# Routing in two segments instead of three, with the value sums, the stores of x and the small steps rearranged, in a fused attention and expert kernel

## The chip, the cores and the metric

The kernel runs on one core of a Trainium2 chip. Its engines work side by side, each through its own list of instructions in order: TensorE (PE, whose weight loads the profile calls PEld), VectorE (DVE), ScalarE (ACT), GpSimd (POOL) and SyncE (SP, which issues most transfers here). The metric is the device time of one execution in microseconds (us). Of the kernel before, three timed runs are given.

## What is computed

Attention over a local window and block summaries, and behind it a mixture of eight experts. The core of the reference (B = 4 batches, H = 8 heads, S = 768 positions, head size 64, so rows of 512):

```python
k_sum = k.reshape(B, H, nb, block, D).max(axis=3)      # blocks of 32
v_sum = v.reshape(B, H, nb, block, D).mean(axis=3)
scores_l = scale * q @ k.T, kept where |i - j| < 16
scores_s = scale * q @ k_sum.T + log(32)
a = softmax(concat(scores_l, scores_s))
x = a @ concat(v, v_sum)                               # 4 x 768 rows of 512
for b, s in order:
    fresh_e = argmax(x[b, s] @ w_gate)
    e = fresh_e if s == 0 or sigmoid(x[b, s] @ w_local) < 0.5 else prev_e
    p = softmax(x[b, s] @ w_gate)
    out[b, s] = p[e] * (relu(x[b, s] @ w1[e]) @ w2[e])
```

A row's expert can be that of the row ahead of it, so a routing scan runs through each batch. With the given inputs all 768 rows of batch 0 go to one expert, those of batch 1 to a second, batch 2 and most of batch 3 to a third (1400 rows), 135 to a fourth and one row to a fifth: 24 blocks of up to 128 rows, and two small remainders.

## The kernel before, in words

**Attention.** The 32 pairs of heads and batches are cut into 16 head pairs n (4 batches by 4) with two groups g each, so 32 groups G, G = 2n + g, and `attention` runs a software pipeline over G. In group G PE makes the scores (`s_mm`, L300 and L306, into two banks of PSUM called bs), then in odd groups the gate's product of the values (`gate_v`, L265), in even groups its transposes (`gate_t`, L273), then the transposes of the probabilities of group G - 2 (`t_stage`, L326), and the value product of group G - 3 (`a_mm`, L337, into the one bank ba). The sums of the values over blocks are a small product too (`sum_v`, L251): from n = 2 on it is made in even groups and written to spare columns of the scores' bank, copied by ACT to vs (L253) and spread by POOL into the value tile vw (`spread_v`, L258). DVE takes the maximum of the scores (nm, L312), block maxima or block sums of the next k or v (L218, L222), and normalizes: `a_norm` writes dn and xs (L352, L353), which empties ba. ACT makes the exponentials (L316) and copies. POOL also copies windows of k (L244), folds the next v (`fold_v`, L229) and scales summaries (L247).

**Loads and stores.** SP issues the loads of kp, q, vt and vw in program order, two or three pairs ahead. When the fourth head pair of a batch is normalized, `a_norm` also has SP store the rows of x to `x_dram` (L357), two stores of 876 KB a batch. The store waits for xs, and what follows on SP waits behind it.

**Small steps.** Routing is a chain of small instructions, written as generators that yield before each: "DVE", "LONG" (a large DVE step), "PE" or "PE late" (a product), "ACT", "WAIT". `later` puts a chain in the list `steps`; `small(n)`, called three times in each group with 3, 2 and 4, takes that many steps, PE's only after two or four calls since the step ahead. Behind attention `flow` does the same by a model of time.

**Routing.** `SEG` cuts the batches in three segments: 0, then 1 and 2, then 3. `route(k)` finds each row's expert (L539 to L579), counts and ranks (L582 to L606), and makes the selection matrix A (L626). It runs for segment 0 from group 10 on, for segment 1 from group 26 on, for the last behind attention. `early(j)` picks two blocks of 128 rows each ahead of the rest: j = 0 from batch 0, j = 1 and 2 from batches 0 to 2, all of expert e0, the one with the most rows in batch 0; j = 3 is for e1, which `second` chooses. `gate_p` makes the rows' weights, with one exponential on ACT between DVE steps (L697 to L702). `finish` places the remaining blocks, makes the list `words` (which expert each slot needs, L1001 and L1006) and the row numbers (L932), first for slots 8 to 11 and then for the rest, and the weights by row (L1023).

**Experts.** Slots are blocks of rows; `pair` runs two blocks of one expert: 96 products for the first layer (L1159 to L1161), 48 for the second (L1078 to L1080), each number in two parts. The first four pairs are the early blocks. The weights of e0 are fetched and split in attention's last groups (wst, L1032, L1036, L1039, L1044); those of e1 are fetched behind attention (stg), and split in the second layer of the third pair. Rows come by an indirect transfer (`gather`, L1050) and are transposed (L1061) into xT.

## Time and profile before

| | |
|---|---|
| median of 3 runs | 459.29 us (458.85 to 460.34) |
| the profiled execution | 458.1 us |
| its span, first to last instruction | 456.3 us |
| mean granted clock of PE | 0.979 |
| busy PE, DVE, POOL, ACT | 418.9, 233.8, 197.3, 183.1 us |
| moved by DMA | 91.28 MB, 200 GB/s over the span |
| attention, up to the first expert product | 137.74 us |
| experts, up to the last product | 440.7 us |

Busy times of an engine are shares of the span in which an instruction of it runs; matmuls overlap, so PE can be busy without being at its peak. In the rows below a time is counted from the span's start; an instruction's row names what it writes and reads (out<-in), and in brackets the idle time of its engine ahead of it with what ended that.

### The profile page before, as it was taken

How to read it: one execution, taken by the hardware profiler on the slowest of the kernel's cores; microseconds unless marked ns; L12 is line 12 of the kernel's file. 1: busy time of each engine (PE TensorE's matmuls, PEld its weight loads, DVE VectorE, ACT ScalarE, POOL GpSimd, SP SyncE). 2: the span in 40 equal slices, each digit the busy share in tenths (PEclk: the TensorE clock that was granted, in tenths of full speed). 3: DMA queues.
4: the chain of work that ended last, by engine and by line, in shares of the span. 5: the costliest groups of instructions: out<-in, count | busy, mean ns of one | idle time of the engine just before them, and what ended most of it. 6: DMA issues, size and time to landing. Idle time of an engine off the chain costs nothing. (4 is left out here: it accounts for less than half of the span.)

```text
span 456.3 us, 11758 instructions
## 1 busy us (share of the span) xinstructions
PE 418.9 (92%) x4329; PEld 358.0 (78%) x4329; DVE 233.8 (51%) x559; ACT 183.1 (40%) x470; POOL 197.3 (43%) x288
## 2 busy tenths in 40 slices
PE   7799898987879999999999999999999999999960
PEld 7577676675658889898989888798988989898840
DVE  4667789797688866668221222226322721214520
ACT  3978776765774222137222111016313721204510
POOL 4497676675574320208621211205820931112930
PEclk9999999989999999999999999999999999999995
DMA  8998998979846470202993246201951671120680
GB/s 306 417 381 311 386 351 264 412 287 337 319 134 218 158 310 1 82 19 87 338 406 115 75 178 225 86 15 28 322 186 39 224 252 70 28 76 25 198 302 32
DMA packets 22854, 91.28 MB, mean 200 GB/s; under 512 B 2767, under 2 KB 3281, under 8 KB 19185
## 3 DMA queue, kind: packets, MB, share of 16 engines
q1 hardware_dynamic: 18176, 74.63, 44.0%
q0 software_dynamic: 4448, 15.42, 10.3%
q8 instruction: 41, 0.67, 0.6%
q14 instruction: 45, 0.36, 0.3%
q10 hardware_dynamic: 144, 0.20, 0.1%
HBM read 76.77 MB, written 13.60 MB: 198 GB/s over the span
## 5 line engine op out<-in xcount | busy, mean ns | idle before, releaser
L1159 PE MATMUL bs<-xT,h 128*128 128x256 f32 x352 | 101.0, 287 | 0.0
L1160 PE MATMUL bs<-xT,h 128*128 128x256 f32 x352 | 99.8, 283 | 0.9 <-DVE xT L1056 0.9
L1161 PE MATMUL bs<-xT,l 128*128 128x256 f32 x352 | 99.6, 283 | 0.0
L1050 POOL DMA_INDIRECT xg<-x_dram,gidx x30 | 32.9, 1096 | 107.5 <-PE bt L1061 39.6
L1078 PE MATMUL ba<-h,hT 128*128 128x512 f32 x176 | 71.5, 406 | 0.3
L1165 ACT ACTIVATE hT<-bs 128x512 fp32r<-128x512 f32 x44 | 26.3, 597 | 112.8 <-PE bs L1161 110.8
L1167 DVE SCALAR_TENSOR_TENSOR hT<-bs,hT 128x512 fp32r<-128x512 f32 x44 | 30.4, 691 | 78.5 <-ACT hT L1165 67.3
L1080 PE MATMUL ba<-h,hT 128*128 128x512 f32 x176 | 68.9, 391 | 0.0
L1079 PE MATMUL ba<-l,hT 128*128 128x512 f32 x176 | 68.8, 391 | 0.0
L1160 PEld LDWEIGHTS bs<-xT,h 128*128 128x128 f32 x352 | 67.4, 192 | 1.7 <-DVE xT L1056 1.4
L1159 PEld LDWEIGHTS bs<-xT,h 128*128 128x128 f32 x352 | 67.4, 191 | 1.8 <-issue 1.2
L1161 PEld LDWEIGHTS bs<-xT,l 128*128 128x128 f32 x352 | 67.4, 192 | 0.2 <-DVE l L1039 0.2
L316 ACT ACTIVATE pr<-bs,nm 128x120 f32<-128x120 f32 x192 | 52.1, 383 | 29.1 <-DVE nm L312 29.0
L1091 POOL DMA_INDIRECT out_dram<-yo,sidx x24 | 25.9, 1078 | 62.1 <-DVE yo L1090 22.2
L1044 POOL TENSOR_TENSOR l<-stg,h 128x256 fp32r<-128x256 f32 x48 | 41.7, 901 | 8.2 <-ACT h L1036 7.6
L258 POOL COPY vw<-vs 24x438 f32<-24x438 f32 x64 | 36.0, 602 | 10.3 <-ACT vs L253 8.3
L337 PE MATMUL ba<-vw,pt 121*64 121x74 f32 x768 | 33.2, 235 | 6.3 <-DVE xs L353 3.8
L312 DVE TENSOR_REDUCE nm<-bs 128x6 f32<-128x720 f32 x32 | 28.7, 900 | 19.6 <-ACT vs L253 18.3
L1080 PEld LDWEIGHTS ba<-h,hT 128*128 128x128 f32 x176 | 33.0, 188 | 7.3
L1078 PEld LDWEIGHTS ba<-h,hT 128*128 128x128 f32 x176 | 33.1, 188 | 6.9 <-ACTq L1330 0.6
L337 PEld LDWEIGHTS ba<-vw,pt 121*64 121x64 f32 x768 | 28.4, 140 | 12.2 <-issue 4.7
L1079 PEld LDWEIGHTS ba<-l,hT 128*128 128x128 f32 x176 | 33.2, 189 | 5.6
(269 smaller groups left out, 658.1 us busy)
## 6 DMA issues: line engine op xcount, KB each, us to landing
stg<-in_w SPq DMA_DIRECT2D x20, 1024.0 KB, 7.6
vw<-in_vW SPq DMA_DIRECT2D x16, 888.0 KB, 7.6
raw<-in_w SPq DMA_DIRECT2D x8, 1024.0 KB, 7.2
x_dram<-xs SPq DMA_DIRECT2D x8, 876.0 KB, 4.8
kp<-in_kT SPq DMA_DIRECT2D x16, 384.0 KB, 5.9
q<-in_qT SPq DMA_DIRECT2D x16, 384.0 KB, 6.9
vt<-in_vT SPq DMA_DIRECT2D x16, 384.0 KB, 7.4
wst<-in_w SPq DMA_DIRECT2D x8, 512.0 KB, 5.8
```

The source lines that it names most:

```text
L258: nc.gpsimd.tensor_copy(out=vf[n % 3][WL:W, t:t + NW // 4, 1:1 + PW], in_=vs.to_broadcast([NB, NW // 4, PW]))
L316: nc.scalar.activation(out=pr[:, h, u, :], in_=sp[:, h, u, :], func=AF.Exp, bias=nm[:, h, u:u + 1], scale=1.0)
L337: nc.tensor.matmul(out=ap[64 * c:64 * c + 64, u, h, :], lhsT=pt[0:W + 1, h, u, 64 * c:64 * c + 64], rhs=vw[n % 3][0:W + 1, 2 * (NG * g + u ...
L1044: eng.tensor_tensor(out=lo[:, p], in0=src[:, p], in1=hi[:, p].bitcast(F32), op=ALU.subtract)
L1050: self.nc.gpsimd.indirect_dma_start(out=t.rearrange("p a d -> p (a d)"), out_offset=None, in_=rows, in_offset=bass.IndirectOffsetOnAxis(ap ...
L1078: nc.tensor.matmul(out=ps, lhsT=ah, rhs=wh, start=first, stop=False)
L1079: nc.tensor.matmul(out=ps, lhsT=ah, rhs=wl, start=False, stop=False)
L1080: nc.tensor.matmul(out=ps, lhsT=al, rhs=wh, start=False, stop=last)
L1159: nc.tensor.matmul(out=ps[:, j], lhsT=wh, rhs=xh, start=(k == 0), stop=False)
L1160: nc.tensor.matmul(out=ps[:, j], lhsT=wh, rhs=xl, start=False, stop=False)
L1161: nc.tensor.matmul(out=ps[:, j], lhsT=wl, rhs=xh, start=False, stop=(k == KT - 1))
L1167: nc.vector.scalar_tensor_tensor(out=l, in0=ps, scalar=0.0, in1=h.bitcast(F32), op0=ALU.max, op1=ALU.subtract)
```

## The change

- **Two segments.** `SEG` is batch 0, then batches 1 to 3. `early` is one chain for six blocks (EARLY = 6), all of e0 and all from batch 0, with one product for their row numbers and one for their weights. `second`, `early_p`, e1 and the first part of the row numbers are gone; the next expert's weights are fetched when `words` are there, and slots from 6 on are ordinary ones. The route of batches 1 to 3 starts behind attention, followed at once by `finish`.
- **Value sums.** From n = 2 on the product is made in odd groups, behind the gate's product and into the same bank; ACT copies both.
- **Stores of x.** `a_norm` notes the store; it is issued one group later, behind that group's loads (for the last batch in the same group).
- **Small steps.** `small` takes a budget in us: for even groups 0.5, 0.2 and 0.3, for odd ones 0.7, 0.4 and 0.3, from group 28 on 0.9, 0.5 and 0.4. A step costs 0.29, a LONG one 0.95, PE, ACT and WAIT 0.1. "ACT" waits four calls like "PE late", and both routes use "PE late".

```diff
-SEG = ((0, 1), (1, 3), (3, 4))
+SEG = ((0, 1), (1, B))
-EARLY = 8
-FIRST = 12
+EARLY = 6
-ON_PE = {"PE": 2, "PE late": 4}
+ON_PE = {"PE": 2, "PE late": 4, "ACT": 4}
+TIME, MORE = ((0.5, 0.2, 0.3), (0.7, 0.4, 0.3), (0.9, 0.5, 0.4)), 28
...
             def gate_v(n):
...
+                sums = m[:, 256:256 + 2 * DG]
+                if n > 1:
+                    sum_mm(n, sums)
                 gs = gss[n] = wk.tile([P, GW], F32, name="gs", bufs=2)
                 nc.scalar.copy(out=gs, in_=m[:, 0:GW])
+                if n > 1:
+                    sum_copy(n, sums)
...
                 if p == NP - 1:
                     t = b * NU + NG * g
-                    nc.sync.dma_start(out=self.x_dram[:, t:t + NG, :], in_=x.rearrange("p u a d -> p u (a d)"))
+                    stores.append((G + LA + (0 if b == B - 1 else 1), t, x))
...
-                if 2 * GP < G < last_g and g == 0 or G == 2 * GP + 1:
-                    sum_v(n, spare)
...
                 if G < last_g:
                     s_exp(G)
-                    self.small(3, True)
+                    self.small(TIME[groups[G][1] if G < MORE else GP][0], True)
...
+                while stores and stores[0][0] <= G:
+                    _, t, x = stores.pop(0)
+                    nc.sync.dma_start(out=self.x_dram[:, t:t + NG, :], in_=x.rearrange("p u a d -> p u (a d)"))
                 tick(G, 5)
                 tick(G, 1)
...
-            self.credit -= 4 if head[0] == "LONG" else 1
+            self.credit -= 0.95 if head[0] == "LONG" else 0.1 if head[0] in ON_PE or head[0] == "WAIT" else 0.29
...
-        on_pe = "PE late" if k == 0 else "PE"
+        on_pe = "PE late"
...
-        yield from rows(EARLY, FIRST)
...
         self.have_words()
-        yield from rows(FIRST, COLS)
-        yield from self.gate_p(B - 1, B)
-        yield from self.until(*(("weights", b) for b, _ in SEG[:2]))
+        yield from rows(EARLY, COLS)
+        yield from self.gate_p(*SEG[1])
...
-        after = ([self.early(0), self.also(self.early_p(*SEG[0], 0))],
-                 [self.early(1), self.early(2), self.also(self.early_p(*SEG[1], 1, 2, 3)), self.second()])
-        for k in range(NS - 1):
-            at(GP * NP * SEG[k][1] + 2, 1, lambda k=k: self.later(self.route(k), *after[k]))
+        at(GP * NP * SEG[0][1] + 2, 1, lambda: self.later(self.route(0), self.early()))
...
             def have_words():
                 st["words"] = reg(COLS + EARLY - 2, (ENG.SP,), E - 1)
-                refills()
+                for w in range(2):
+                    refill(w, st["words"])
```

Three places of the order. SP around the two stores of batch 0's rows, before and after:

```order
L186 DMA vw_144<-in_vW 128x1776
L357 DMA x_dram<-xs 128x3x584
L174 DMA kp_136<-in_kT 128x768
L182 DMA q_133<-in_qT 128x768
L357 DMA x_dram<-xs 128x3x584
L178 DMA vt_140<-in_vT 128x768
L186 DMA vw_142<-in_vW 128x1776
```

```order
L182 DMA vw_139<-in_vW 128x1776
L170 DMA kp_131<-in_kT 128x768
L178 DMA q_128<-in_qT 128x768
L174 DMA vt_135<-in_vT 128x768
L182 DMA vw_137<-in_vW 128x1776
L452 DMA x_dram<-xs 128x3x584
L170 DMA kp_130<-in_kT 128x768
L178 DMA q_129<-in_qT 128x768
L452 DMA x_dram<-xs 128x3x584
L174 DMA vt_136<-in_vT 128x768
```

Each store (x_dram) stood ahead of the loads of its group; now it stands behind the loads of the next group.

DVE in groups 26 and 27, before and after (nm is the maximum of the scores that opens a group on DVE; l_all collects the gate's inputs):

```order
L359 TENSOR_REDUCE l_all<-xs 128x27
L539 TENSOR_REDUCE mx_2186<-l_all 128x12
L542 TENSOR_TENSOR eq_2192<-l_all,mx_2186 128x96
L544 TENSOR_TENSOR eq_2192<-eq_2192,c_82 128x96
L547 TENSOR_REDUCE rv_2195<-eq_2192 128x12
L312 TENSOR_REDUCE nm<-bs 128x6
L550 TENSOR_TENSOR sv_2197<-c_82,rv_2195 128x12
L553 SCALAR_TENSOR_TENSOR val_2242<-l_all,sv_2197 128x12
L555 COPY val_2242<-sv_2197 1x2
```

```order
L321 TENSOR_REDUCE nm<-bs 128x6
L663 TENSOR_REDUCE gmx_2153<-l_all 128x6
L666 TENSOR_TENSOR ex_2201<-l_all,gmx_2153 128x48
L218 TENSOR_REDUCE va<-vf 128x24
L361 RECIPROCAL dn<-ba 128x6
L362 TENSOR_TENSOR xs<-ba,dn 128x3x146
L321 TENSOR_REDUCE nm<-bs 128x6
L671 TENSOR_REDUCE sm_2204<-ex_2201 128x6
L673 TENSOR_SCALAR sm_2204<-sm_2204 128x6
L214 TENSOR_REDUCE ks<-kp_131 128x24
L361 RECIPROCAL dn<-ba 128x6
```

The second route's first four steps stood between l_all and nm of group 27; now one step of batch 0's early blocks stands there, and its exponential's sum (L671) comes a group behind the input of it (L666).

PE around the product for `words` (L1001 before, L947 after), in the second pair of the experts:

```order
L1080 MATMUL ba_3465<-h_118,hT 128x512
L1078 MATMUL ba_3465<-h_118,hT 128x512
L1079 MATMUL ba_3465<-l_120,hT 128x512
L1080 MATMUL ba_3465<-h_118,hT 128x512
L1001 MATMUL bt<-ident,w_3501 1x46 x2
L1159 MATMUL bs<-xT,h_117 128x256
L1160 MATMUL bs<-xT,h_117 128x256
L1161 MATMUL bs<-xT,l_119 128x256
L1159 MATMUL bs<-xT,h_117 128x256
```

```order
L1104 MATMUL bs<-xT,h_112 128x256
L1105 MATMUL bs<-xT,h_112 128x256
L1106 MATMUL bs<-xT,l_114 128x256
L947 MATMUL bt<-ident,w_3082 1x46 x2
L1104 MATMUL bs<-xT,h_112 128x256
L1105 MATMUL bs<-xT,h_112 128x256
L1106 MATMUL bs<-xT,l_114 128x256
L1104 MATMUL bs<-xT,h_112 128x256
L1105 MATMUL bs<-xT,h_112 128x256
```

It stood behind the last product of the second pair (ba); now it stands ahead of that pair's second layer, six products before the end of the first (bs).

## Rows read from the trace of the kernel before

**Rows 1.** Busy us (instructions) of each engine by stage, TensorE clock, DMA share, GB/s
```profile
29.24:42.43 13.19, 13.00 (x262) 10.05 (x259) 9.70 (x18) 11.05 (x42) 11.51 (x23) 1.00 0.88 314
42.43:84.52 42.09, 37.41 (x729) 28.52 (x726) 36.05 (x88) 30.66 (x117) 26.53 (x52) 1.00 0.94 342
84.52:105.24 20.72, 18.21 (x331) 14.30 (x328) 16.14 (x40) 13.96 (x54) 16.84 (x31) 0.92 0.84 323
105.24:125.52 20.28, 15.61 (x270) 11.86 (x267) 14.48 (x33) 13.21 (x44) 9.91 (x18) 0.92 0.90 341
125.52:137.74 12.22, 9.64 (x165) 7.43 (x162) 10.79 (x27) 9.07 (x27) 8.61 (x11) 1.00 0.39 131
137.74:240.19 102.45, 101.55 (x803) 91.45 (x800) 64.41 (x237) 31.00 (x45) 35.47 (x37) 1.00 0.50 182
```

**Rows 2.** PE timeline, clean groups: start us, busy us, instructions, idle before and its releaser
```profile
29.24 0.35 PE L300 MATMUL bs<-me 64*64 64x360 bf16 x4
...
34.55 0.43 PE L251 MATMUL bs<-wgi,va 128*24 128x146 f32 x2
...
42.43 0.35 PE L300 MATMUL bs<-me 64*64 64x360 bf16 x4
```

**Rows 3.** PE timeline, the same columns: long waits of attention
```profile
75.35 1.00 PE L337 MATMUL ba<-vw,pt 121*64 121x74 f32 x24 [1.20 <-DVE xs L353]
...
92.60 1.75 PE L337 MATMUL ba<-vw,pt 121*64 121x74 f32 x24 [1.31 <-DVE xs L353]
...
111.34 0.27 PE L558 MATMUL bt<-ident,val 128*12 128x128 f32 x1 [2.73 <-DVE val L555]
```

**Rows 4.** DVE timeline: the gate's sum, behind ACT
```profile
90.13 0.20 DVE L702 TENSOR_REDUCE sm<-ex 128x6 f32<-128x48 f32 x1 [1.60 <-ACT ex L698]
```

**Rows 5.** Stages again, columns as in group 1, behind PE's two long waits
```profile
92.00:96.00 4.00, 3.40 (x55) 3.06 (x56) 3.76 (x11) 1.38 (x6) 3.83 (x9) 0.57 0.98 366
112.00:116.00 4.00, 4.00 (x44) 3.00 (x38) 1.14 (x3) 1.77 (x7) 0.66 (x2) 0.57 1.04 422
```

**Rows 6.** SP's DMA issues: a store of x and the next load
```profile
44.57 0.38 SPq L357 DMA_DIRECT2D x_dram<-xs  x1
45.04 0.44 SPq L178 DMA_DIRECT2D vt<-in_vT  x1
```

**Rows 7.** POOL timeline: the fold of the next values, the last spread
```profile
51.44 1.16 POOL L229 TENSOR_TENSOR vf<-vt 128x192 f32<-128x192 f32 x2 [3.48 <-DMA vt<-in_vT]
...
132.37 3.69 POOL L258 COPY vw<-vs 24x438 f32<-24x438 f32 x4
```

**Rows 8.** A stage with DMA at its fastest, columns as in group 1
```profile
53.00:56.30 3.30, 2.85 (x61) 2.61 (x62) 2.35 (x6) 2.85 (x12) 2.58 (x6) 1.00 1.06 435
```

**Rows 9.** Who waited for whom: us in total, times, longest
```profile
DVE nm L312 <- ACT vs L253: 18.3, 12, 2.9
```

**Rows 10.** PE timeline: a wait in attention's tail
```profile
133.90 0.60 PE L337 MATMUL ba<-vw,pt 121*64 121x74 f32 x10 [0.45 <-POOL vw L258]
```

**Rows 11.** PE timeline: starts of an expert pair without routing and of its successor
```profile
381.03 0.28 PE L1159 MATMUL bs<-xT,h 128*128 128x256 f32 x1
...
404.42 0.28 PE L1159 MATMUL bs<-xT,h 128*128 128x256 f32 x1
```

**Rows 12.** PE by line, first four expert pairs: count, busy us, mean ns, idle
```profile
L775 PE MATMUL bt<-ebp,A 128*128 128x6 bf16 x54 | 1.8, 166 | 0.0
L746 PE MATMUL bt<-ebt,A 128*128 128x4 bf16 x54 | 1.8, 165 | 0.0
L932 PE MATMUL bt<-bt,A 128*128 128x8 bf16 (+1 forms) x48 | 1.7, 180 | 0.0
```

**Rows 13.** DVE timeline: the last route's first step, and the words
```profile
140.90 0.20 DVE L539 TENSOR_REDUCE mx<-l_all 128x6 f32<-128x48 f32 x1
...
191.25 0.24 DVE L1006 CAST words<-bt 1x92 int32<-1x92 f32 x1 [2.18 <-PE bt L1001]
```

**Rows 14.** ACT timeline: the first cast of fetched expert weights
```profile
204.38 1.04 ACT L1036 CAST h<-stg 128x1024 fp32r<-128x1024 f32 x1
```

## The prediction

> **What bounds the kernel now.** I read the stages first [rows 1]. From 137.74 us to 440.7 us TensorE multiplies for the experts without a pause (101.55 busy in 102.45 us of the first four pairs), so that part shrinks only by work that PE loses. The 15.6 us behind it are the last rows' way out; nothing there is touched. Before 137.74 us stands attention, 32 groups. Where nothing disturbs it, PE is the bound there too: group 7 starts at 29.24 and group 11 at 42.43, four groups in 13.19 us, 3.30 us each, with 13.00 us of PE busy [rows 1, 2]. From group 11 on it is slower. Against 3.30 us a group, the stretch 42.43 to 84.52 (11 groups) is 5.8 us too long, 84.52 to 105.24 (5 groups) 4.2, 105.24 to 125.52 (4 groups) 7.1. The last stretch, 125.52 to 137.74, would cost 9.0 us without waits (a group of 3.3 and, an estimate at the same pace, 5.7 for what is left of three more groups and the first expert transposes); it takes 12.2, 3.2 too many. In all 20.3 us of excess [rows 1], and this is what the change can win in attention.

> Who is late in it? PE's waits show it [rows 3]: the value products wait for DVE's xs (1.20 us at 75.35, 1.31 us at 92.60), since one bank holds them and DVE must empty it first; the transpose of val stands at 111.34 after 2.73 us, for a DVE step of the second routing. Behind DVE is routing: DVE is busy 9.70 of 13.19 us in the clean stretch, 36.05 of 42.09 us in the next, 9.4 us above the clean rate (0.735 of 36.3 us), just what 11 groups leave free (0.265 of 36.3 is 9.6). At 90.13 DVE also stands 1.60 us for the gate's exponentials on ACT [rows 4]. After the two long waits PE's clock is granted at 0.57, one stretch of 4 us each [rows 5], which loses 0.43 of 4, some 1.7 us; those slow groups belong to the 4.2 and the 7.1.

> **Part by part.** *Routing in two segments.* Of the work between groups 26 and 31, the route of batches 1 and 2 goes to the time behind attention. In its place stays the tail of batch 0's chain, which the order shows now ending in group 31. So the stretch of 7.1 loses the 2.73 us wait and the 1.7 us of slow clock behind it, and the PE steps of that route; what stays is the splitting of the weights, with four casts on ACT and one long subtraction on DVE in the last groups. I leave 2.5 of 7.1 (bounds 0, if ACT has room, and 7.1, if casts were the whole cause; nearer to the low end, since 4.4 have names that go).

> *Small steps in us.* Before, nine steps fit in a group; now 1.0 us in even and 1.4 us in odd groups (1.8 from group 28 on), at 0.29 us a step: three or four, and five. Batch 0's route and early blocks took 9.4 us of DVE above the clean rate up to 84.52 and 4.0 (16.14 less 0.735 of 16.5) up to 105.24, 13.4 in all; spread over the 20 groups from 11 to 30, that is 0.67 us a group against 0.87 free. DVE thus stays behind PE instead of in front of it. Of the 5.8 I leave 2.0: 1.2 us for the chain's own 18 products on PE (twelve like L775 at 1.8 / 54 = 0.033 us [rows 12], the other six at 0.13, an estimate between that and the 0.27 of the one at 111.34 [rows 3]) and 0.8 of waits; bounds 1.2 and 5.8. Of the 4.2 I leave 0.5, since the wait for ACT gets four calls of distance and the clock has no reason to fall; bounds 0 and 4.2.

> *Stores behind loads.* Now the store waits on SP for xs and holds vt's load behind it: issued at 44.57 and 45.04 [rows 6], landed when POOL, 3.48 us idle, folds it at 51.44 [rows 7]. Afterwards loads go first and the store waits for nothing. I price it at nothing by itself: PE's long waits name DVE, not a transfer. The cover is the distance from the fold to the products that need it, and POOL's slack, 1.68 us in the clean 13.19; without it the bound would be the 3.48 us for each of three batches, 10.4. The traffic fits: the clean stretch moves 314 GB/s at a share of 0.88 [rows 1], stores add 0.9 MB twice in 26.4 us, 66 GB/s, to 380, and up to 435 GB/s are seen [rows 8].

> *Value sums beside the gate's product.* The two matmuls move from even to odd groups, 0.36 us of PE either way (0.43 busy, next work 0.36 later [rows 2]), and write into the gate's bank. nm no longer waits for ACT's copy of vs, which was 18.3 us in 12 waits [rows 9]. I price this at nothing: 34.55 in rows 2 is such a group, and PE runs on at 3.30 us with that wait inside. Bounds: 0 and the 1.5 us for each of 12 groups. [...] The trace has the wait and no PE idle behind it, so the row decides.

> *Tail.* POOL spreads the last sums at 132.37 in 3.69 us, after its share of the weights, and PE waits for it at 133.90 [rows 7, 10]. The order leaves this as it is: I keep 3.0 of 3.2 (bounds 0 and 3.2).

> Attention thus keeps 2.0 + 0.5 + 2.5 + 3.0 = 8.0 of 20.3 us: 12.3 us gained.

> *Behind attention.* A pair without routing takes 23.39 us (381.03 to 404.42) [rows 11]; the first four take 102.45, 8.9 more, of which 0.9 is the first wait for xT. The rest is routing's own matmuls and what each breaks. The change drops there all of L775 and L746, 108 products and 3.6 us of PE, and the narrower of the two sets of 24 in L932, which take 1.7 together and that one some 0.7 [rows 12]; the route and the wide products stay. That is 4.3, less 0.1 for wider products: 4.2 us gained (bounds 3.6, if the sets merge at the cost of both, and 8.0, all of the excess but the wait). The three new early pairs use the weights that are there; the fourth needs the next expert's. Its fetch now follows the words. In the order the words' product stands six products ahead of the second layer of the second pair, some 35.7 us into the stage (25.0 for the first pair, 90 products at 0.12); the first cast of fetched weights comes, as now, in the second layer of the third pair (204.38 is 66.6 us in, after the change some 61) [rows 14]. 25 us for four megabytes, 11 at 380 GB/s: no wait.

> **Sum.** The profiled execution took 458.1 us, a span of 456.3 and 1.8 around it, 1.2 below the median of the runs. 458.1 - 12.3 - 4.2 = **441.6 us**.

> **Rivals.** *(a) Attention stays bound by DVE, ACT or DMA.* The steps per group are fewer, but in groups 28 to 31 the budget rises while ACT casts, and the same bytes go through in less time. For it: DVE works at 86% of the span from 42.43 on, and DMA shares of 0.94 in that stretch. Against it: 0.67 us against 0.87 free, and 314 GB/s where the clean pace is held. If only the second routing's waits go (4.4 us) and 1 us elsewhere, 458.1 - 5.4 - 4.2 = 448.5 us.

> *(b) The other side: PE waits in line for the single routing chain.* PE takes its work in order, so a words' product that stands 35.7 us into the stage stops the experts if DVE's chain is not done. Now 50.4 us pass from the first step of that chain to the words (140.90 to 191.25) [rows 13]. At that pace from 3 us on it is done at 53.4; PE stands 17.7 us, and slow clock behind such a wait adds 1.7: 441.6 + 19.4 = 461.0 us, slower. It decides from a chain of 33 us on, a microsecond for each microsecond. Against it: three early chains and a second choice of expert were interleaved with it and are gone, and the DVE steps that the order lists ahead of the words, at their durations in the trace, sum to about 34 us from the start of the stage, other work of the experts among them.

> *(c) The stores do count.* Then up to 10 us of attention are won by that part instead of by the steps; the excess is the same, and its floor is 1.2 us: 458.1 - 19.1 - 4.2 = 434.8 us.

> **How the numbers follow.** Forecast 0.72, (a) 0.16, (b) 0.06, (c) 0.06. The range reaches nearly to (c), and 2 us past (a), for casts that cost all of the 7.1: 435.5 to 451. Outside it are (b) and the far ends. A measurement of this kernel tells some 0.3% from no change (458.85 to 460.34 in three runs). Faster 0.92 (forecast, a, c, less some of a's far end), same 0.03, slower 0.05.

> **What would show it.** Right: groups 11 to 27 at 3.3 to 3.5 us and no clock of 0.57; PE's wait for val gone; the first expert product some 12 us earlier; the first four expert pairs near 98 us; no PE wait at the words. Wrong: value products still waiting for xs (steps), POOL still waiting for vt with PE idle behind it (stores), PE idle ahead of the words' product (b), or a DMA share of 1 through the last twelve groups.

## The result, and the profile after

The changed kernel takes 445.89 us (444.76 to 447.59), the kernel before 459.07 us in the same comparison: a ratio of 0.9722, 95% interval 0.9671 to 0.9774. That is 13.2 us less where 16.5 were forecast. The profiled execution took 444.76 us, a span of 443.0 and 1.8 around it, 13.3 less than the one of before. Of these, 10.1 lie ahead of the first expert product and 3.4 between it and PE's last product; the way out is 0.3 longer.

The stages of the kernel after, in the windows that begin with the same groups as [rows 1]; columns as there:

```profile
29.24:42.06 12.82, 12.82 (x262) 10.34 (x259) 9.70 (x17) 11.32 (x44) 11.37 (x24) 1.00 0.96 355
42.06:80.22 38.16, 36.17 (x724) 28.64 (x721) 31.06 (x74) 31.41 (x117) 27.26 (x55) 1.00 1.00 367
80.22:97.82 17.60, 16.07 (x328) 13.22 (x325) 15.20 (x36) 14.09 (x54) 13.03 (x26) 1.00 0.98 374
97.82:115.66 17.84, 13.47 (x264) 10.49 (x260) 13.42 (x33) 12.38 (x45) 10.81 (x20) 1.00 1.00 370
115.66:127.60 11.94, 9.92 (x172) 7.85 (x169) 8.66 (x18) 9.72 (x30) 9.09 (x13) 1.00 0.53 169
127.60:227.79 100.19, 98.89 (x678) 88.73 (x674) 60.90 (x162) 30.24 (x43) 36.78 (x38) 1.00 0.50 188
```

The clock is 1.00 in every stretch, where [rows 5] had 0.57. DVE is busy 31.06 us of the second stretch instead of 36.05. The DMA share, 0.84 to 0.94 before, is now 0.98 to 1.00 in the middle of attention: the same bytes go through in less time.

PE's timeline of two groups that nothing disturbs, the counterpart of [rows 2]:

```profile
42.06 0.35 PE L309 MATMUL bs<-me 64*64 64x360 bf16 x4
42.24 0.79 PE L315 MATMUL bs<-kb,q 64*64 64x120 f32 x24
42.95 0.59 PE L268 MATMUL bt<-vt,wg 128*32 128x224 f32 x8
43.35 0.41 PE L247 MATMUL bt<-wgi,va 128*24 128x146 f32 x2
43.70 0.87 PE L335 MATMUL bt<-ident,pr 128*120 128x128 f32 x6
44.50 1.00 PE L346 MATMUL ba<-vw,pt 121*64 121x74 f32 x24
45.42 0.35 PE L309 MATMUL bs<-me 64*64 64x360 bf16 x4
...
48.36 0.35 PE L309 MATMUL bs<-me 64*64 64x360 bf16 x4
```

An odd group takes 3.36 us and an even one 2.94: 6.30 us a pair, where before each took 3.30. The forecast held the clean pace for fixed; it is not.

Waits of the kernel after, from 29 to 128 us: who waited for what, us in total, times, longest:

```profile
DVE xs L362 <- DMA x_dram<-xs: 7.7, 3, 3.3
...
ACT pr L325 <- DVE nm L321: 4.0, 3, 3.3
...
POOL vf L225 <- DMA vt<-in_vT: 2.5, 2, 1.5
```

POOL's wait for V, one of whose cases is in [rows 7], was 11.5 us in all from 29 to 138 us in the kernel before; it has shrunk to 2.5, and that of [rows 9] is gone. But the first line is new: the normalisation that writes a tile of x waits until an earlier store of x has landed. One of the three, on DVE, then ACT, then PE:

```profile
109.39 0.62 DVE L362 TENSOR_TENSOR xs<-ba,dn 128x438 f32<-128x438 f32 x1 [3.31 <-DMA x_dram<-xs]
```

```profile
112.43 1.62 ACT L325 ACTIVATE pr<-bs,nm 128x120 f32<-128x120 f32 x6 [3.26 <-DVE nm L321]
```

```profile
110.26 1.00 PE L346 MATMUL ba<-vw,pt 121*64 121x74 f32 x24 [1.72 <-DMA wst<-in_w]
...
114.73 1.00 PE L346 MATMUL ba<-vw,pt 121*64 121x74 f32 x24 [1.46 <-DVE p L686]
```

The value products share DVE's lateness: their bank is free only when xs is written (109.39 and 0.62 on). The trace puts the first of the two down to another DMA. Ahead of the second, DVE also has work of its own: the long subtraction of the fetched weights (109.92, 1.59 us) and the gate's small steps.

In the expert part, the first product and the start of the fifth pair:

```profile
127.60 0.38 PE L1104 MATMUL bs<-xT,h 128*128 128x256 f32 x1
...
227.79 0.28 PE L1104 MATMUL bs<-xT,h 128*128 128x256 f32 x1
```

### The profile page after: what moved, and what is told of

It is laid out like the page before. It is cut to its first block, busy times and chain, and to the rows that moved or that the text cites. A ratio compares the mean times of both kernels' runs of the same rounds, so it can differ in the third digit from the quotient of the medians.

```text
span 443.0 us, 11507 instructions
## 1 busy us (share of the span) xinstructions
PE 409.0 (92%) x4190; PEld 352.5 (80%) x4190; DVE 223.3 (50%) x455; ACT 182.9 (41%) x467; POOL 196.9 (44%) x288
## 5 line engine op out<-in xcount | busy, mean ns | idle before, releaser
L1036 POOL DMA_INDIRECT out_dram<-yo,sidx x24 | 25.8, 1077 | 72.7 <-DVE yo L1035 25.3
L989 POOL TENSOR_TENSOR l<-stg,h 128x256 fp32r<-128x256 f32 x48 | 42.9, 924 | 7.4 <-ACT h L981 7.4
L261 POOL COPY vw<-vs 24x438 f32<-24x438 f32 x64 | 33.6, 564 | 23.3 <-ACT vs L251 10.0
L346 PE MATMUL ba<-vw,pt 121*64 121x74 f32 x768 | 32.1, 231 | 4.0 <-DMA wst<-in_w 1.7
L981 ACT CAST h<-stg 128x1024 fp32r<-128x1024 f32 x32 | 32.7, 1050 | 7.0 <-PE ba L1025 6.3
L346 PEld LDWEIGHTS ba<-vw,pt 121*64 121x64 f32 x768 | 27.3, 136 | 9.3 <-issue 6.3
```

The source lines that it names most:

```text
L261: nc.gpsimd.tensor_copy(out=vf[n % 3][WL:W, t:t + NW // 4, 1:1 + PW], in_=vs.to_broadcast([NB, NW // 4, PW]))
L346: nc.tensor.matmul(out=ap[64 * c:64 * c + 64, u, h, :], lhsT=pt[0:W + 1, h, u, 64 * c:64 * c + 64], rhs=vw[n % 3][0:W + 1, 2 * (NG * g + u ...
L981: self.nc.scalar.copy(out=hi, in_=src)
L989: eng.tensor_tensor(out=lo[:, p], in0=src[:, p], in1=hi[:, p].bitcast(F32), op=ALU.subtract)
```

## Experiments

The start of the kernel is not the same in each execution: group 7 begins between 28.8 and 32.2 us in these profiles. So each profile is read from the start of group 7. The table has, for each run, the ratio to the kernel before, the time from group 7 to the start of group 30, and from group 7 to the first expert product. Without a disturbance the first of these would be 12 x 3.36 + 11 x 2.94 = 72.7 us (75.9 with 3.30 for every group). The difference of two ratios in the table is known to about 3 us either way, by their intervals.

| kernel | us | ratio | 95% | 7 to 30 | 7 to experts |
|---|---|---|---|---|---|
| before | 459.07 | 1 | | 91.4 | 108.5 |
| changed | 445.89 | 0.9722 | 0.9671 to 0.9774 | 82.0 | 98.4 |
| routing alone | 448.72 | 0.9785 | 0.9737 to 0.9832 | 86.7 | 104.6 |
| changed, steps by count | 449.75 | 0.9802 | 0.9771 to 0.9833 | 87.1 | 101.5 |
| changed, sums back | 449.11 | 0.9805 | 0.9760 to 0.9850 | 86.6 | 103.6 |
| changed, stores back | 442.61 | 0.9655 | 0.9614 to 0.9696 | 77.4 | 98.1 |
| four x buffers | 442.54 | 0.9643 | 0.9600 to 0.9685 | 80.4 | 95.8 |
| register read late | 444.21 | 0.9685 | 0.9637 to 0.9733 | 82.7 | 100.4 |
| four buffers, mixed stores | 442.38 | 0.9675 | 0.9628 to 0.9721 | 79.9 | 95.0 |
| four buffers, half a block | 439.14 | 0.9592 | 0.9538 to 0.9646 | 76.2 | 93.9 |
| four buffers, a whole block | 441.26 | 0.9645 | 0.9600 to 0.9690 | 80.4 | 95.7 |
| four buffers, fewer loads | 439.35 | 0.9601 | 0.9545 to 0.9657 | 76.2 | 92.5 |
| half a block alone | 443.23 | 0.9690 | 0.9646 to 0.9734 | 79.6 | 97.4 |
| four together | 438.67 | 0.9571 | 0.9541 to 0.9600 | 76.7 | 92.4 |

**The four parts of the change.** Three runs each undo one part, and one leaves the routing alone. Routing alone: sums in the score bank, stores ahead of the loads and steps by count.

> The changed routing in two segments with the early blocks from batch 0, and the other three parts undone: value sums in the score bank, stores ahead of the loads, small steps by count. By the forecast's own sum the routing and the step budget carry the whole gain, the other two nothing: with the budget undone 444 to 448 us (0.970 to 0.977). By the runs so far the sums are worth 4 us, the stores cost 3, and the experts gain 4.4 us whatever the attention does: the routing alone then gives 447 to 450 us (0.976 to 0.983), with clean pairs of 6.6 us.

448.72 us, 0.9785: 2.15% less than before, 9.8 us of 458, as the second expectation had it. Steps by count in the changed kernel:

```diff
-self.small(TIME[groups[G][1] if G < MORE else GP][0], True)
+self.small(3, True)
...
-self.credit -= 0.95 if head[0] == "LONG" else 0.1 if head[0] in ON_PE or head[0] == "WAIT" else 0.29
+self.credit -= 4 if head[0] == "LONG" else 1
...
```

> The changed kernel with the small steps by count, as before (3, 2 and 4 to an iteration, a long one for four, no delay of the steps on ACT), and nothing else undone. Theory A, what the other runs leave for the budget: the routing alone gave 0.9785, the sums 4 us, the stores cost 2.5 to 3 us, so the budget is worth 1 to 2 us: 446 to 447.5 us on a kernel before of 458 us (0.974 to 0.977). Theory B, what the forecast leaves for it (16.5 us less the routing's 9.8): 6 to 7 us, 451 to 452 us (0.986).

Between the two: 0.9802 against 0.9722, 3.7 us for the budget together with ACT's four calls. The forecast's cause is seen in it: PE's timeline of this run has waits like those of [rows 3], where DVE has small steps ahead of its normalisation, at 79.49 those of the early blocks and at 97.93 those of the gate's weights. They come to 3.5 us in three places, of the 5.1 us that groups 7 to 29 are longer. DVE also stands for ACT's exponentials again, as in [rows 4], 1.46 us at 91.15.

```profile
79.49 1.00 PE L346 MATMUL ba<-vw,pt 121*64 121x74 f32 x24 [1.43 <-DVE xs L362]
...
97.93 1.00 PE L346 MATMUL ba<-vw,pt 121*64 121x74 f32 x24 [1.45 <-DVE xs L362]
```

The value sums at their old place:

```diff
+if 2 * GP < G < last_g and g == 0 or G == 2 * GP + 1:
+    sum_v(n, spare)
...
-sums = m[:, 256:256 + 2 * DG]
-if n > 1:
-    sum_mm(n, sums)
...
```

> The changed kernel with the value sums back at their old place, in the score bank of the even groups, and nothing else undone. Theory A, the sum's product is almost free behind the gate's product and costs 0.30 us at the old place, in 13 groups: 4 us more, 449 to 450 us (0.979 to 0.981 of the kernel before), and a clean pair of groups of 6.6 us in place of 6.3. Theory B, as the forecast had it, the move is worth nothing: 445 to 446.5 us, pairs of 6.3 us.

0.9805 against 0.9722: 3.8 us, as the first expectation had it. PE's timeline of a clean pair in this run:

```profile
36.35 0.43 PE L247 MATMUL bs<-wgi,va 128*24 128x146 f32 x2
36.71 1.00 PE L340 MATMUL ba<-vw,pt 121*64 121x74 f32 x24
37.63 0.35 PE L303 MATMUL bs<-me 64*64 64x360 bf16 x4
...
38.52 0.59 PE L267 MATMUL bt<-vt,wg 128*32 128x224 f32 x8
39.04 0.87 PE L329 MATMUL bt<-ident,pr 128*120 128x128 f32 x6
40.01 1.00 PE L340 MATMUL ba<-vw,pt 121*64 121x74 f32 x24
40.93 0.35 PE L303 MATMUL bs<-me 64*64 64x360 bf16 x4
```

In the even group the sum costs 0.36 us (36.35 to 36.71). In the odd group without it, the transposes begin 0.52 us after the gate's products and the value products 0.97 after that. With it (42.95 to 44.50 above) the steps are 0.40, 0.35 and 0.80: 1.55 instead of 1.49. So the sum costs 0.06 us there, 0.30 less, 13 times.

The stores at their old place:

```diff
-stores.append((G + LA + (0 if b == B - 1 else 1), t, x))
+nc.sync.dma_start(out=self.x_dram[:, t:t + NG, :], in_=x.rearrange("p u a d -> p u (a d)"))
```

> The changed kernel with the stores of x at their old place, ahead of the loads of their iteration, and nothing else undone. Theory A: DVE's three waits for x stores go (4 to 6 us back), and SP's waits ahead of the K, Q and V loads come back (POOL's wait for V at the groups after a store, some 1 to 2 us in each of three places): the two nearly cancel, 443 to 447 us. Theory B, the forecast's upper bound, the deferral is worth much: 10 us more, 456 us. Theory C, the deferral was worth nothing and cost nothing: 445 to 446 us with the same waits on DVE.

442.61 us, a little better than the first expectation: with the stores put off the kernel takes 3.1 us longer (0.9722 against 0.9655). The three waits for x stores are gone. Groups 7 to 29 gain 4.6 us, but this run loses 5.0 at once in group 30 (9.48 us against 4.47), where SP issued the last V load behind the store of batch 2, at 98.67 where the changed kernel issued it at 93.70:

```profile
98.20 0.38 SPq L366 DMA_DIRECT2D x_dram<-xs  x1
98.67 0.47 SPq L174 DMA_DIRECT2D vt<-in_vT  x1
```

```profile
110.66 1.48 PE L315 MATMUL bs<-kb,q 64*64 64x120 f32 x24 [3.97 <-POOL kb L243]
```

The V loads of that stretch took 9.0 us to land (median), and POOL folds and summarises only then, from 109.06 us on:

```profile
vt<-in_vT SPq DMA_DIRECT2D x2, 384.0 KB, 9.0
```

So the deferral does what it says there; what it made besides was the wait for a buffer. From group 7 to the first expert product the two nearly cancel (98.1 us against 98.4). The 2.3 us by which the two profiles differ lie elsewhere for the most part: 1.0 in the first expert pair (25.06 us against 26.04, as short in the run with four buffers, where the stores are put off too) and 0.8 behind PE's last product. So it is not shown that the 3.1 us are the price of the buffer.

These four numbers, 9.8, 3.7, 3.8 and -3.1, add up to 14.2 us; the whole gave 12.7 (2.78% of 458), which the intervals allow.

**The x buffers.** Three tiles hold x; the fourth tile's turn comes back to the first, two groups after that one's store is now issued. This run has four:

```diff
-xs[b, g] = wk.tile([P, NG, NP, PW], F32, name="xs")
+xs[b, g] = wk.tile([P, NG, NP, PW], F32, name="xs", bufs=4)
```

> The changed kernel with four buffers for the x tiles in place of three (the high halves of the second weights, 16 KB, are allocated at the end of the attention to make room). In the profile of the changed kernel DVE's normalisation waited 7.7 us, three times, until an x store had landed. Theory A, the deferred stores made a new wait, because the third buffer is wanted two groups after its store is issued: the three waits go, the groups behind them come back to their clean 2.9 to 3.4 us, and the time falls by 4 to 6 us, to 440 to 442 us (0.958 to 0.963 of the kernel before). Theory B, the waits stand beside other late work (ACT, loads) and cost little: under 1 us, 445 to 446 us (about 0.970).

442.54 us: 3.6 less than the changed kernel by the ratios, between the two expectations; in the profiles 2.6 of it lie ahead of the experts and 1.0 in the first expert pair. The waits are gone; 80.4 us from group 7 to 30 is still 7.7 above the clean pace. What is left is not DVE: on PE's timeline, two rows each of groups 27 and 29:

```profile
99.84 0.57 PE L315 MATMUL bs<-kb,q 64*64 64x120 f32 x11
102.44 0.63 PE L315 MATMUL bs<-kb,q 64*64 64x120 f32 x13 [2.03 <-issue]
...
108.58 0.37 PE L315 MATMUL bs<-kb,q 64*64 64x120 f32 x7
109.49 0.72 PE L315 MATMUL bs<-kb,q 64*64 64x120 f32 x17 [0.53 <-issue]
```

PE stops in the middle of 24 like products and waits for nothing that the trace shows. Counting PE's records (products, weight loads, its other instructions) from the first, every gap of over 0.4 us between starts, from 55 to 110 us, stands at a number of one row (a gap holds the usual step too, so PE's idle time is less: 2.03 of the 2.29 above):

```
record   1985   2497   2753   3009   3265   3521   3777
gap us   0.43   1.36   0.70   0.73   0.48   2.29   0.79
apart           512    256    256    256    256    256
```

The gaps of the changed kernel at 2497, 2753, 3009, 3521 and 3777 (0.86, 1.31, 1.61, 1.20, 0.51 us) are of the same row. At 3009 its trace puts a wait down to ACT's pr, which is a wrong lead: the next run looked for the cause ahead of it.

**The register read.** In the changed kernel SP reads the first expert's number as soon as the step is issued and stands until it is there. Here the read waits for the first weight fetch.

```diff
 def wfetch(j):
+    if "e0" not in st:
+        st["e0"] = nc.values_load(self.e0[0:1, 0:1], engines=(ENG.SP,), min_val=0, max_val=E - 1)
...
 def have_e0():
-    st["e0"] = nc.values_load(self.e0[0:1, 0:1], engines=(ENG.SP,), min_val=0, max_val=E - 1)
```

> The changed kernel with the register read of the first early expert on SP put off to the first weight fetch, so that SP no longer stands before the K and Q loads of iteration 21 to 22. In the changed kernel SP issued nothing from 75.8 to 80.9 us. Theory A, these late loads are what made groups 22 and 23 long (8.0 us against 6.3 for a clean pair): the K load is issued 4 to 5 us earlier, and the time falls by 1 to 2 us, to 444 us (0.967). Theory B, the long group there is ACT's and DVE's own work for the first routing segment: no change, 445 to 446 us.

SP's loads in the kernel after and then in this run:

```profile
75.50 0.33 SPq L182 DMA_DIRECT2D vw<-in_vW  x1
80.89 0.33 SPq L170 DMA_DIRECT2D kp<-in_kT  x1
```

```profile
77.77 0.33 SPq L182 DMA_DIRECT2D vw<-in_vW  x1
78.20 0.81 SPq L170 DMA_DIRECT2D kp<-in_kT  x1
```

The load goes earlier, and group 23 is as long as before (4.87 against 4.94 us), with its wait at the same instruction:

```profile
87.31 0.59 PE L268 MATMUL bt<-vt,wg 128*32 128x224 f32 x8 [1.47 <-ACT pr L325]
```

That is record 3009 again. 82.7 us from group 7 to 30 against 82.0, and 1.7 us less by the ratios, well inside the intervals: no effect is shown.

**Code in blocks.** If PE's instructions arrive in blocks of 256, then 128 instructions ahead of everything must move the gaps by 128 in the program, into the even groups.

```diff
-WARM = 44
+WARM = 108
-nc.tensor.matmul(out=wb[:, 0:P], lhsT=self.wz, rhs=self.wz, start=True, stop=True)
+nc.tensor.matmul(out=wb[:, 0:48], lhsT=self.wz, rhs=self.wz[:, 0:48], start=True, stop=True)
```

> The changed kernel with four x buffers, and 64 more warm-up products (128 more PE instructions) ahead of everything, each of 48 columns so that the warm-up is not much longer. In the run with four x buffers every PE gap of over 0.4 us between 55 and 110 us stands at PE record number 1985, 2497, 2753, 3009, 3265, 3521 or 3777, that is at distances of 256 or 512, always in an odd group. Theory A, PE's code comes in blocks of 256 instructions and the block is late: the gaps stay at the same record numbers and so fall 128 instructions earlier in the program, in the even groups, and the odd groups become clean (3.4 us). Theory B, these are waits for other engines that the trace does not name (each pair's work is alike, about 264 records): the gaps stay at the same lines of the odd groups, at numbers 128 higher. The time is the same by both within the start's spread, 440 to 445 us (0.960 to 0.968).

PE's timeline, an even group and the odd one behind it:

```profile
79.84 0.78 PE L315 MATMUL bs<-kb,q 64*64 64x120 f32 x23
81.08 0.31 PE L315 MATMUL bs<-kb,q 64*64 64x120 f32 x1 [0.46 <-issue]
...
84.27 0.59 PE L268 MATMUL bt<-vt,wg 128*32 128x224 f32 x8
84.67 0.41 PE L247 MATMUL bt<-wgi,va 128*24 128x146 f32 x2
```

The gap at 81.08 is at record 3009 (0.72), another at 3521 (0.80). Two more, at 2161 (0.42) and 3767 (0.75), are not of the row; they too are in even groups, at score products, and the second is put down to POOL's kb. The odd groups from 15 to 29 are clean, 3.36 us but for one of 3.50. So the two gaps that are left kept their numbers and left their lines, and the other five fell below 0.4 us: the first theory holds. The time, 439.14 us, was better than expected. Moved by a whole block (172 products of 16 columns):

> Four x buffers and 128 further warm-up products (256 PE instructions, each of 16 columns). Theory A, the code comes in blocks of 256 instructions and what counts is where the border falls: moved by a whole block, the borders are back at the lines of the odd groups where they are without a shift; PE's gaps of over 0.4 us stand there again, and groups 7 to 29 take 80 to 81 us as with four buffers alone, against 76.2 us with the half block. Theory B, a longer warm-up helps, or shifting as such: groups 7 to 29 take 76 to 78 us. The start may be 1 to 2 us later for the warm-up, so the time is 440 to 445 us by either.

```profile
71.01 0.41 PE L247 MATMUL bt<-wgi,va 128*24 128x146 f32 x2 [1.01 <-issue]
78.37 0.38 PE L268 MATMUL bt<-vt,wg 128*32 128x224 f32 x2 [0.89 <-issue]
...
99.28 0.63 PE L315 MATMUL bs<-kb,q 64*64 64x120 f32 x13 [1.48 <-issue]
```

These are records 2753, 3009 and 3777, in odd groups again, and 80.4 us from group 7 to 30, as without a shift: neither the longer warm-up nor the shifting as such helps.

The borders also enter the comparisons above. At the six from 2497 to 3777 PE stood 4.2 us in the changed kernel, 4.6 with the sums back, 5.8 with the steps by count and 1.8 with the stores back. So 1.6 us of what the steps by count lose, and 2.4 of the 4.6 that groups 7 to 29 gain with the stores back, are stops for code and not the waits named there.

That the block is late because of the loads was tried with a kernel that leaves out some of them, the values of the last six pairs:

```diff
-if 1 < n + 1 < N:
+if 1 < n + 1 < 10:
     load_w(n + 1)
```

> The changed kernel with four x buffers, without the loads of vW (888 KB each) for the last six pairs, so that the values of those pairs are wrong: 40% of the bytes of a pair are not moved from 65 us on. Theory A, the code blocks are late because they queue with the loads on the DMA engines: the gaps at record numbers 2497 to 3777 (6.3 us in all in the run with four x buffers) fall below 2 us in all, groups 20 to 29 fall from 36.9 us to 32 to 33 us, and the time by 4 to 6 us, to 437 to 439 us (0.954 to 0.958). Theory B, the gaps come from engines that are late by their own work: the gaps stay, and the time moves by under 1.5 us.

439.35 us, near the first expectation. The same groups, 23 to 29, with all loads and then with fewer (columns as in [rows 1]):

```profile
85.60:112.61 27.01, 23.57 (x464) 18.61 (x461) 22.10 (x50) 20.76 (x75) 20.12 (x38) 1.00 1.00 371
```

```profile
82.43:105.59 23.16, 22.70 (x465) 18.11 (x463) 21.62 (x48) 20.72 (x75) 19.86 (x37) 1.00 0.84 294
```

3.9 us less in these seven groups, and none of the gaps of over 0.4 us at 3009 to 3777 is left; at 2497, before the light part begins to tell, 1.37 us still stands, and 0.42 at 2753. The shift in the changed kernel with its three buffers:

> The changed kernel with the 64 further warm-up products alone (three x buffers, as changed). Theory A, what the shift gains is the place of the code blocks' borders, in even groups where PE and the others have slack, and this adds to the x buffers: the three waits of DVE for x stores stay, the odd groups are else clean, 441 to 443 us (0.963 to 0.967). Theory B, the shift gained nothing by itself and the shifted run was a lucky start: 445 to 446 us (0.972).

443.23 us, between the two: the three waits stay (6.2 us), while PE stands 0.5 us at the six borders instead of 4.2. 2.4 us less from group 7 to 30, but 1.5 less in the time, which the intervals don't separate from nothing.

**Two tries for a better kernel.** Stores of batches 0 and 1 at the old place, those of batch 2 put off, with four buffers:

> The changed kernel with four x buffers, with the stores of batches 0 and 1 at the old place (ahead of the loads) and those of batch 2 deferred. In the run with all stores at the old place groups 7 to 29 took 77.4 us, against 80.4 us with four buffers and all stores deferred, and then one group lost 6 us to a V load that SP issued late behind the store of batch 2. Theory A, for batches 0 and 1 the old place is no worse, and it was the store of batch 2 whose deferral paid: 438.5 to 441 us (0.957 to 0.962). Theory B, the 3 us were chance in where the code blocks were late: as with four buffers, 442 to 443 us (0.964).

442.38 us, the second theory: with four buffers no difference is shown by where these stores stand. Then four buffers, the half block, the late register read, and `MORE` at 99, which takes the larger budget from the last groups:

> Four x buffers, the 64 further warm-up products, SP's register read put off to the first weight fetch, and the larger step budget of the last four groups taken away (DVE had the routing's small steps ahead of its maximum in group 30, where PE waited 1.6 us). Theory A: the wait in group 30 goes, 1 to 1.5 us less than with four buffers and the shift: 437.5 to 439 us (0.956 to 0.959). Theory B, the steps put off there stand in the tail and are late for the first pair's store: no gain, 439 to 440 us (0.959 to 0.961).

438.67 us, 0.9571 (0.9541 to 0.9600): the fastest here, faster than both kernels. PE's timeline in group 30, first with four buffers and the half block alone, then in this run:

```profile
111.11 1.00 PE L346 MATMUL ba<-vw,pt 121*64 121x74 f32 x24 [1.56 <-DVE p L686]
```

```profile
107.29 0.84 PE L315 MATMUL bs<-kb,q 64*64 64x120 f32 x23 [0.88 <-issue]
...
109.61 1.00 PE L346 MATMUL ba<-vw,pt 121*64 121x74 f32 x24 [0.36 <-DVE p L686]
```

The wait for DVE has shrunk by 1.2 us as expected, but the group is as long as before (4.57 us against 4.56): in its place PE stops 0.88 us at record 4033, 256 on from the last of the row. The step from 439.14 to 438.67 is too small to tell.

## Why the prediction was right, and where it missed

**Attention: 12.3 us forecast, 10.1 measured.** By stretch, as the forecast cut it:

| groups | before | forecast | after |
|---|---|---|---|
| 11 to 21 | 42.09 | 38.3 | 38.16 |
| 22 to 26 | 20.72 | 17.0 | 17.60 |
| 27 to 30 | 20.28 | 15.7 | 17.84 |
| tail | 12.22 | 12.0 | 11.94 |

The first is right in size by luck. At the pace that the change itself brought, 6.30 us a pair, groups 11 to 21 would take 34.9 us and keep 3.3 of waits where the forecast left 2.0; the gain in pace hid the difference. The last is right in size too, though PE's longest wait there is now for ACT (1.60 us at 122.53) and not for POOL's spread. The step that failed is the 2.5 us left in groups 27 to 30: they kept 4.6 (17.84 - 13.2). Against the new pace (12.6 us for these four groups) it is 5.2. Group 27 is 1.4 too long, with a late code block at 3521. Group 29 is 2.4 too long, with DVE's wait of 3.31 us for an x store and a block at 3777. Group 30 is 1.5 too long, where PE waits 1.46 us behind DVE's subtraction and small steps. This last wait stays without the other two (1.56 us with four buffers and the half block, where the subtraction comes 1.26 us late for ACT's cast), and with the steps by count group 30 takes 2.93 us. I had left room for casts on ACT only, and that room covers group 30; the buffer and the code were the rest.

**Stores priced at nothing.** Mis-sized, in the sign too: 3.1 us lost, though only 0.3 of it is seen between group 7 and the experts. What was missed is a wait, 7.7 us of DVE in three places, that is gone with a fourth tile and with the stores back. I looked at what the store holds behind itself on SP and not at what it holds by being late, the tile of x. The sentence "the store waits for nothing" was true of the store; the next but two tile waits for it. POOL's wait for V fell from 11.5 us to 2.5, and group 30 of the run with stores back shows the one place where putting them off counted, 5.0 us.

**Value sums priced at nothing.** Mis-sized: 3.8 us gained. I compared PE's own time for the two products at both places, 0.36 us, and not what the following products cost behind them. As forecast, the wait of nm for ACT's copy, 18.3 us in all [rows 9], ended without PE gaining as much: the sums' whole worth is a fifth of that.

**Steps in us.** Right in kind: with counts, PE waits for DVE's xs at 79.49 and 97.93 as in [rows 3]; with the budget it does not. The budget is worth 3.7 us and the routing 9.8, together 13.5 where the forecast put the whole 16.5 on them. So two terms that I had set to zero, +3.8 and -3.1, nearly cancel, and that they do is luck; the main term was 3.0 too large, as far as the intervals let it be told.

**Behind attention: 4.2 us forecast.** The profile shows 3.4 (302.5 to 299.1 from the first expert product to PE's last). In the runs where the first pair took 25.05 us instead of 26.04 it is 4.4 (298.1 with four buffers, with these and the half block, and with the sums back). The difference is one wait in the first pair of the changed kernel, for the transpose of the second route's val:

```profile
133.01 0.27 PE L563 MATMUL bt<-ident,val 128*18 128x128 f32 x1 [0.83 <-DVE val L560]
```

This is rival (b) at 0.8 us instead of 19.4: the single chain is waited for once, at its start, and not at the words, where PE runs on (its product starts at 164.68, the one ahead at 164.47). Weights came in time: from 127.60 to 227.79 us PE's waits name val (0.8 us) and xT (0.5 us) alone. The small products went as forecast (of those in the first four pairs, all of L775 and L746 and 24 of L932 are gone), but the first four pairs took 100.19 us, not near 98: products that stood in the fifth pair are now in the fourth, and 1.1 of the 3.4 us lie behind the fourth pair.

**The rivals.** (a), with 448.5, is nearer to the median of 445.89 than 441.6 is, but it gave attention 5.4 us, where 10.1 were gained and the forecast had 12.3. Its sign of a DMA share of 1 through the last groups was there. What fell short was mostly a buffer and code; DVE and ACT held PE up in group 30, for 1.5 us. With four buffers and the half block attention was faster at a share of 1.00 still. (c) fell with the stores' sign. The clock fell nowhere in attention, as said (1.00 in each stretch). "Groups 11 to 27 at 3.3 to 3.5" was wrong: clean groups were faster, others 3.9 to 4.9.

**Open.** Why the border of a block costs less in the even groups at no less traffic (396 GB/s in groups 23 to 29 with four buffers and the half block, 371 with four buffers alone) is not settled. Nor was it tried to move loads in time so that a block finds a gap between them.

## What to carry to other kernels

A transfer that is put off keeps its source (DVE waited 7.7 us here for tiles of x): before moving a store back, count when its buffer is written next, and give it one more if it is in the same few steps. Price a small product at its new place by the time from the product ahead to the one behind, with and without it (0.36 us at the old place, 0.06 at the new). PE's stops in the middle of like products, 256 records or a multiple of it apart and up to 2.03 us long, were code that came late here; shifting the program by half a block (0.5 us at the six borders instead of 4.2), or thinning the loads (none of over 0.4 us left at 3009 to 3777), told them apart from waits.

## What the runs showed of the hardware that I had not expected

```profile
q8 instruction: 40, 0.66, 0.6%
```

```profile
q8 instruction: 5, 0.08, 0.9%
```

These are 40 packets of 16,384 bytes; between the gaps lie 256 records or a multiple of it. The trace has the time of each packet. In the run with four buffers, the end of the packet ahead of a stop and the start of PE's record behind it (us):

```
record      2497   2753   3009   3265   3521   3777
landed     72.20  79.15  85.81  92.38 101.08 108.01
PE goes on 73.62  80.43  87.21  93.77 102.44 109.49
```

In all fourteen kernels every gap of over 0.4 us at a number of the row, from 55 to 110 us, ends 1.2 to 1.6 us after a packet of q8 has landed (the five of the changed kernel 1.30 to 1.45 us), and PE passes none of the borders from 1985 to 4033 sooner than 1.2 us after one. With fewer loads the packets for 3009 to 3777 landed 2.1 to 4.3 us ahead, and PE did not stop. So the packets of q8 are PE's code, and the stops are waits for it.

The time of the stops: with four buffers, at 365 GB/s and a share of 0.99 from group 7 to 30, PE stood at the six borders from 2497 on for 1.01, 0.34, 0.66, 0.22, 2.03 and 0.53 us, 4.8 us in all.

A wait that the trace names can be one of these: at record 3009 it names ACT's pr in the changed kernel (1.53 us), in the run with the late read (1.47) and, by 256 further on, in the run with a whole block (0.66), and the count of records shows that all three are the border.
